# Seven tiles for raw weights in place of three, and one weight load ahead of queries and keys

## The chip, the cores and the metric

One core of a Trainium2 chip runs the whole kernel in one launch. The metric is the device time of a launch in microseconds (us); a lower time is better. The engines are named as in the profile: PE (TensorE matmul), PEld (its weight load), DVE (VectorE), ACT (ScalarE), POOL (GpSimd) and SP (SyncE, which here only issues DMAs).

## The reference, cut to what matters

```python
x = attention(rotate(q), rotate(k), v)        # 4 batches, 8 heads, 576 tokens, 64 wide
x = x.transpose(0, 2, 1, 3).reshape(2304, 512)
h = x @ w_in                                  # 512 x 2048, float64 in memory
x = np.maximum(0.01 * h, h) @ w_out           # 2048 x 512, float64 in memory
idx, gate = route(x, expert_emb, tau)         # one of 8 experts for each token
out = gate * (np.maximum(x @ w1[idx], 0) @ w2[idx])
```

The change concerns `w_in` and `w_out` alone: 16 MB of 64-bit numbers that must be turned into 32-bit ones and then into pairs of 16-bit halves (a high part and a low part) before the dense layer can use them.

## The kernel before, in words

**Stages.** Attention runs over 16 pairs of heads (`g`), nine steps each, 144 steps in all. In steps 0 to 35 (`g` below `WHOLE`, batch 0) a step works in 32 bits: DVE takes the row maximum (L621), ACT the exponential (L626), PE transposes the result (L645), ACT and DVE copy it out (L651, L655), PE multiplies it with the values (L679), and on some steps PE runs filler matmuls (`keep_warm`, L659). Steps 36 to 143 use 16-bit halves and the dense layer is worked in between: 72 units, each a first matmul (`m_s1`, L285), a leaky ReLU (L292 to L303) and a second matmul (`m_s2`, L315). A unit takes two steps, one in the order `ORDER_A`, one in `ORDER_B`. What is left of the dense layer after step 143 runs alone, and the experts follow.

**Weights.** `w_in` and `w_out` are cut into 16 slices of 1 MB (`slices`, L208), taken in turn from the two. A job `weights(i)` (L210) owns a home tile: it issues the slice's DMA on SP (L215 or L224), decodes with two ACT and two DVE pieces (`decode`, L198, L200, L202, L205), squares it on ACT (L230 or L219) and, for a slice of `w_in`, sums over partitions on PE (L191), takes a power of two on DVE (`_pow2`, L91 to L93) and makes the halves (ACT L236, DVE L238). A slice of `w_out` decodes into `wo32` instead and keeps no halves yet. Then the job takes the next slice into the same home, whose DMA waits until the last instruction on that home is done. There are `NW + 1` = 3 homes: two tiles `raw0`, `raw1`, and the tile that later holds `xT`. When all 16 are squared, `convert` (L242) finds the scale of `w_out`, sets `M.known`, and two jobs `parts` make the halves of `w_out` in eight parts (ACT L261, DVE L263). A unit of the dense layer waits for the parts that it reads (`m_ready`, L267), and the rows of attention are made into 16 bits (`x_done`, L718) only once `M.known` is set and the job on the `xT` home is done.

**Order.** The program order of every engine is written out by a planner at build time. Each engine works its own list in that order. Jobs yield pieces with a cost on ACT (`A`) or DVE (`V`); a step has a few slots, and a slot goes through the jobs in a fixed list: rows to finish, the preparation of the next pair of heads (`prep_whole`, `prep`), values, routing, then the weight jobs by index, then `parts`. Every step adds `RATE1` (A=2.4, V=2.7) to two budgets that are capped at 1.5 times that; a weight piece is planned only while its budget is above zero, and a slot takes no more pieces of an engine once 1.2 of cost are used. After a load, a job's first piece waits for two steps (`TICK`). In the steps of batch 0 a job may not go from ACT to DVE or back within a step. Before step 0 the planner runs six steps without attention (`PRE`), in which only weight work and the routing directions are planned; the rotation of the first queries and keys (`ropes`, L411) is planned at their start.

```python
    em = mp.tile([NE, DM], F32, name="em", tag="x2T", bufs=1)      # L770
    nc.sync.dma_start(out=em, in_=emb)
    for t in range(2):
        load(0, t)                          # queries, rotation table, keys, on SP
    nc.sync.dma_start(out=idn, in_=ident)
    end(load_values(0))                     # values, on SP
    nc.sync.dma_start(out=itau, in_=tau.to_broadcast([128, 1]))
...
    wjobs += [Job(weights(i)) for i in range(NW + 1)]              # L1215
    rjobs.append(Job(directions()))
    M.step = -1
    for _ in range(PRE):
        step(None)
    a_scores(0)
```

Of the kernel before, what the change touches and what calls it, by code (L numbers as in the profile page):

```python
# [9 lines left out]
F32 = mybir.dt.float32  # L10
# [4 lines left out]
U32 = mybir.dt.uint32  # L15
AF = mybir.ActivationFunctionType
# [19 lines left out]
XTB = 2  # L36
NW = 2
# [8 lines left out]
SPARE = 4  # L46
# [39 lines left out]

def _pow2(nc, pool, sq2, n, inv):

    t = pool.tile([128, n], U32, name="pt", tag=f"pt{n}")
    s = pool.tile([128, n], F32, name="ps", tag=f"ps{n}")  # L90
    nc.vector.tensor_scalar(out=t, in0=sq2.bitcast(U32), scalar1=0xFFFFFFFF, scalar2=24, op0=ALU.bitwise_xor, op1=ALU.logical_shift_right)  # L91
    nc.vector.tensor_scalar(out=s.bitcast(U32), in0=t, scalar1=-50.0, scalar2=2.0 ** 23, op0=ALU.add, op1=ALU.mult)
    nc.vector.tensor_scalar(out=inv.bitcast(U32), in0=t, scalar1=-2.0 ** 23, scalar2=304.0 * 2 ** 23, op0=ALU.mult, op1=ALU.add)  # L93
    return s
# [3 lines left out]
def attention_moe_kernel(ctx: ExitStack, tc: tile.TileContext, qkv, w_in, w_out, emb, tau, w1, w2,  # L98
                         rope, ident, tokc, iota, pcol, out):
    nc = tc.nc  # L100
# [5 lines left out]
    small = pool("small", 3)  # L106
# [40 lines left out]
    wo = wq.tile([128, 2, NF, DM], F16, name="wo")  # L147
    wo32 = wq.tile([128, NF, DM], F32, name="wo32")
    homes = [wp.tile([128, 2, 2048], F16, name=f"raw{i}") for i in range(NW)] + [mp.tile([128, 2, 2048], F16, name="xT", bufs=1)]
    blocks = []  # L150
    for b in range(B):
        blocks += [((b, 0), (b, 1)), ((b, 2), (b, 3))]
# [17 lines left out]
    M = Ctx()  # L170
# [13 lines left out]
    def cur_block():  # L184
        return munits[M.unit][0] if M.unit < len(munits) else len(blocks)
# [23 lines left out]

    def weights(i):  # L210
        raw = homes[i].rearrange("p a b -> p (a b)").bitcast(U32).rearrange("p (f t) -> p f t", t=2)
        while len(slices) > (SPARE if i >= NW else 0):
            f, o = slices.popleft()
            if o:
                nc.sync.dma_start(out=raw.rearrange("p (c f) t -> p c (f t)", c=2),  # L215
                                  in_=w_out32[256 * f:256 * f + 256, :].rearrange("(c p) f -> p c f", p=128))
                r = yield from decode(raw, wo32[:, 2 * f:2 * f + 2].rearrange("p c f -> p (c f)"))
                yield Piece(A=1.3)
                nc.scalar.activation(out=wo[:, 0, 2 * f:2 * f + 2].rearrange("p c f -> p (c f)"), in_=r, func=AF.Square, accum_out=uw[:, 1, f:f + 1])  # L219
                M.normed += 1  # L220
                if M.normed == NF // 2:
                    cjobs.append(Job(convert()))
            else:
                nc.sync.dma_start(out=raw.rearrange("p (c f) t -> p c (f t)", c=4),  # L224
                                  in_=w_in32[:, 512 * f:512 * f + 512].rearrange("(c p) f -> p c f", p=128))
                wv = (yield from decode(raw)).rearrange("p (c f) -> p c f", c=4)
                hi, lo = (wi[:, a, :, 256 * f:256 * f + 256] for a in range(2))
                sq = small.tile([128, 1], F32, name="wsq", bufs=NW + 1)
                yield Piece(A=1.3)
                nc.scalar.activation(out=lo, in_=wv, func=AF.Square, accum_out=sq)  # L230
                pb = yield from total(sq, 1)
                yield Piece(must=True, V=0.2)
                s = _pow2(nc, small, pb[:, 0:1], 1, uw[:, 0, f:f + 1])
                M.scaled.add(f)
                yield Piece(A=1.2)
                nc.scalar.activation(out=hi, in_=wv, func=AF.Copy, scale=s)  # L236
                yield Piece(V=1.28)
                nc.vector.scalar_tensor_tensor(out=lo, in0=wv, scalar=s, in1=hi, op0=ALU.mult, op1=ALU.subtract)  # L238
                M.wdone[0].update((2 * f, 2 * f + 1))
            yield Piece()  # L240
# [139 lines left out]
    def decoded():  # L380
        return not slices and not any(z.live for z in wjobs)
# [6 lines left out]
    pairs, values = {}, {}  # L388
# [9 lines left out]

    def load_values(g):
        yield Piece(at=9 * (g - 1) + LAG)  # L400
        v = values[g] = stp.tile([128, 1170], F32, name="v32", tag="v")[:, 0:650].rearrange("p (c h x) -> p c h x", c=5, h=2)
        nc.gpsimd.memset(v[:, :, :, 64:65], 1.0)
        nc.sync.dma_start(out=v[:, :, :, 0:64], in_=qkv[g, :, 2])
        yield Piece()
        if g + 1 < WHOLE:
            vjobs.append(Job(load_values(g + 1)))
        else:
            load(g + 1, 2)
# [309 lines left out]
    def x_done(b, c, x):  # L718

        ch = chunk[b, c]  # L720
        j = block_of[b, c]
        yield Piece(A=0.61, when=lambda: M.known and not any(z.live for z in wjobs[NW:]) and j < cur_block() + (2 * XTB if decoded() else XTB))
        sq = small.tile([128, 1], F32, name="xsq")
        nc.scalar.activation(out=junk[:, 0:512], in_=x, func=AF.Square, scale=2.0 ** 0.5, accum_out=sq, saturate=False)
        yield Piece(V=0.5)
# [43 lines left out]

    em = mp.tile([NE, DM], F32, name="em", tag="x2T", bufs=1)  # L770
    nc.sync.dma_start(out=em, in_=emb)
    for t in range(2):
        load(0, t)
    nc.sync.dma_start(out=idn, in_=ident)
# [437 lines left out]
            slot()  # L1212
            slot()

    wjobs += [Job(weights(i)) for i in range(NW + 1)]  # L1215
    rjobs.append(Job(directions()))
    M.step = -1
    for _ in range(PRE):
        step(None)
# [230 lines left out]
```

## Time and profile before

| | us |
|---|---|
| Median of 3 runs (996.04 to 997.65) | 997.16 |
| The profiled execution, its own time | 999.83 |
| Its span, first to last instruction | 998.0 |
| Start to the first row maximum (step 0, L621) | 37.52 |
| Step 0 to step 36 | 135.16 |
| Step 36 to step 76 | 164.30 |
| Step 76 to the last step, 143 | 267.71 |
| Dense layer alone, then experts | 122.06 and 271.25 |

The profile is of one execution. The span leaves out 1.83 us around it. The stages are cut at the start of a step's row maximum on DVE and read off the timeline; a busy window gives, for a stretch, the busy time of each engine, the TensorE clock granted (1.00 is 2.4 GHz, 0.50 is 1.2 GHz), and the DMA traffic. The name raw in a row stands for `raw0` and `raw1` alike. In a timeline row the brackets hold how long the engine stood idle before the instruction and what ended that.

### The profile page before, as it was taken

The numbers are of one execution on the slowest core, as the hardware profiler recorded it, in microseconds if no ns is written. First come the engines' busy times: TensorE is split into PE (matmuls) and PEld (weight loads), VectorE is DVE, ScalarE is ACT, GpSimd is POOL, SyncE is SP. The second block draws the span as 40 slices with busy tenths as digits, with TensorE's granted clock in tenths as the row PEclk, the third lists the DMA queues.
The fourth block names the chain that finished last, engine by engine and source line by source line (L and its number), as shares of the span: only waits on it lengthen the run. The fifth ranks groups of instructions, "written<-read, shape, count | busy, mean of one in ns | idle before, by whom it ended". The sixth has DMA issues, their size and how long they took to land. (4 is left out here: it accounts for less than half of the span.)

```text
span 998.0 us, 20007 instructions
## 1 busy us (share of the span) xinstructions
PE 908.3 (91%) x7414; PEld 690.6 (69%) x7414; DVE 770.8 (77%) x1601; ACT 671.3 (67%) x1033; POOL 125.5 (13%) x174
## 2 busy tenths in 40 slices
PE   2489888888998889998999999999998999999996
PEld 1377767555776667776677777767666788888885
DVE  4687788699889788888788766332668999999992
ACT  5688788476676676667676656333256998888882
POOL 0000000011201201201101100000013361211110
PEclk9999999799999899999999999999999999999999
DMA  6446333489879968988988854101341111115290
GB/s 208 140 153 208 97 100 76 83 144 173 164 128 149 174 114 154 183 134 142 155 139 138 153 80 81 47 22 33 128 148 44 63 43 43 43 62 193 63 342 20
DMA packets 215607, 118.87 MB, mean 119 GB/s; under 512 B 194727, under 2 KB 195175, under 8 KB 215504
## 3 DMA queue, kind: packets, MB, share of 16 engines
q1 hardware_dynamic: 205648, 84.54, 40.6%
q0 software_dynamic: 9856, 32.99, 12.2%
q8 instruction: 60, 0.98, 0.4%
q14 instruction: 43, 0.35, 0.1%
HBM read 120.04 MB, written 10.49 MB: 131 GB/s over the span
## 5 line engine op out<-in xcount | busy, mean ns | idle before, releaser
L285 PEld LDWEIGHTS <-wi 128*128 128x128 f16 x1920 | 172.6, 98 | 26.2 <-issue 2.7
L315 PE MATMUL acc<-wo,gh 128*128 128x512 f16 x576 | 140.9, 389 | 10.3 <-ACT gh L299 10.3
L292 ACT ACTIVATE g<-h 128x512 f32<-128x512 f32 x72 | 43.0, 598 | 127.5 <-PE h L285 53.8
L626 ACT ACTIVATE E<-E,amx 128x576 f32<-128x576 f32 x144 | 110.5, 767 | 23.8 <-DVE E L621 23.8
L285 PE MATMUL h<-xT,wi 128*128 128x256 f16 (+1 forms) x1152 | 114.4, 258 | 1.1 <-DMA xT<-x 1.1
L621 DVE TENSOR_SCALAR_CACHE_REDUCE E<-S,sc 128x576 f32<-128x576 f32 x108 | 87.9, 814 | 31.7 <-PE S L614 25.1
L315 PEld LDWEIGHTS <-gh 128*128 128x128 f16 x576 | 55.5, 100 | 69.5 <-ACT gh L299 13.0
L285 PE MATMUL h<-raw,wi 128*128 128x256 f16 x768 | 89.1, 273 | 0.0
L630 ACT ACTIVATE P<-E 128x576 f16<-128x576 f32 x108 | 74.0, 685 | 16.5 <-DMA PT<-P 13.3
L634 DVE SCALAR_TENSOR_TENSOR P<-E,P 128x576 f16<-128x576 f32 x108 | 81.1, 751 | 4.4 <-ACT P L630 3.9
L315 PE MATMUL acc<-wo,gl 128*128 128x512 f16 x288 | 76.5, 390 | 1.1 <-DVE gl L303 1.1
L679 PEld LDWEIGHTS <-PT 128*128 128x128 f16 (+1 forms) x1680 | 65.1, 101 | 17.5 <-issue 4.8
L295 DVE SCALAR_TENSOR_TENSOR g<-h,g 128x512 f32<-128x512 f32 x72 | 49.6, 688 | 28.7 <-ACT g L292 28.5
L612 PE MATMUL S<-stk 128*128 128x288 f16 (+1 forms) x240 | 59.0, 289 | 13.2 <-DVE E L621 12.8
L679 PE MATMUL o<-v,PT 128*128 128x65 f16 (+3 forms) x1680 | 69.3, 194 | 1.0 <-DMA PT<-P 1.0
L303 DVE TENSOR_TENSOR gl<-g,gh 128x512 f16<-128x512 f32 x72 | 49.5, 688 | 25.9 <-ACT gh L299 25.7
L1049 PE MATMUL h<-w,hth 128*128 128x512 f32 x176 | 55.4, 396 | 0.4 <-ACT hth L1033 0.4
L315 PEld LDWEIGHTS <-gl 128*128 128x128 f16 x288 | 28.9, 101 | 38.1 <-issue 3.3
L614 PE MATMUL S<-stk,raw 128*128 128x288 f16 (+1 forms) x220 | 52.7, 286 | 0.0
L299 ACT ACTIVATE gh<-g 128x512 f16<-128x512 f32 x72 | 44.5, 618 | 9.9 <-DVE g L295 9.8
L395 POOL DMA_DIRECT2D rawq<-in_qkv x15 | 8.5, 566 | 332.5 <-DVE stg L517 123.8
L983 DVE TENSOR_TENSOR w<-raw,w 128x1024 fp32r<-128x1024 f32 x40 | 46.3, 1221 | 3.5 <-ACT w L982 2.6
(301 smaller groups left out, 2015.7 us busy)
## 6 DMA issues: line engine op xcount, KB each, us to landing
raw<-in_w SPq DMA_DIRECT2D x78, 512.0 KB
ra<-in_w SPq DMA_DIRECT2D x76, 512.0 KB
raw<-in_w_out SPq DMA_DIRECT2D x7, 1024.0 KB
raw<-in_w_in SPq DMA_DIRECT2D x6, 1024.0 KB
rawq<-in_qkv POOLq DMA_DIRECT2D x15, 320.0 KB, 3.5
rawk<-in_qkv POOLq DMA_DIRECT2D x15, 320.0 KB, 6.5
x2s<-x POOLq DMA_DIRECT2D x18, 256.0 KB, 4.4
rawv<-in_qkv POOLq DMA_DIRECT2D x12, 320.0 KB, 3.7
```

The source lines that it names most:

```text
L285: nc.tensor.matmul(m.h[:, c0:c1], lhsT=wi[:, a, c, 128 * f:128 * f + 128], rhs=xT[j][:, 4 * b_ + c, 0:c1 - c0], start=(n == 0), stop=(n == ...
L295: nc.vector.scalar_tensor_tensor(out=m.g, in0=m.h, scalar=0.01 / TWO15, in1=m.g, op0=ALU.mult, op1=ALU.max)
L303: nc.vector.tensor_tensor(out=m.gl, in0=m.g, in1=m.gh, op=ALU.subtract)
L315: nc.tensor.matmul(M.acc[:, t], lhsT=g_[:, tt], rhs=wo[:, a, f], start=(f == 0 and n == 0), stop=(f == NF - 1 and n == 2))
L612: nc.tensor.matmul(ps[o:o + m, n, 0:288], lhsT=stk[:, h, c0:c0 + m], rhs=stk[:, 2 + h, ks], start=True, stop=False)
L614: nc.tensor.matmul(ps[o:o + m, n, 0:288], lhsT=pairs[g][3][:, h, c0:c0 + m], rhs=stk[:, 4, ks], start=False, stop=True)
L621: nc.vector.tensor_scalar(out=e[:, 0:S].rearrange("p (a b) -> p a b", a=2), in0=ps[:, :, 0:288], scalar1=-0.125 if g < WHOLE else pairs[g] ...
L626: nc.scalar.activation(out=e[:, 0:S], in_=e[:, 0:S], func=AF.Exp, scale=-1.0, bias=mx)
L630: nc.scalar.activation(out=p[:, 0:576], in_=e[:, 0:S], func=AF.Copy, scale=TWO15)
L634: nc.vector.scalar_tensor_tensor(out=p[:, 576:1152], in0=e[:, 0:S], scalar=TWO15, in1=p[:, 0:576], op0=ALU.mult, op1=ALU.subtract)
L679: nc.tensor.matmul(o[ob:ob + m, 256 * h:256 * h + r.shape[-1]], lhsT=pt[:, i, q0:q0 + m], rhs=r, start=(n == 0), stop=(n == len(todo) - 1))
L1049: nc.tensor.matmul(OP[kk], lhsT=h_[:, c, :], rhs=wt[a][c // 2][:, 512 * (c % 2):512 * (c % 2) + 512], start=(n == 0), stop=(n == len(todo) ...
```

## The change

- `homes` has seven tiles: the three of before and four views of `wo`, the tile in which the 16-bit halves of `w_out` are put later.
- The job on the first home is made, and its load issued on SP, ahead of queries, table and keys; its two ACT pieces are put at the head of ACT's list by two calls before the planner starts. The other six jobs are made where the three were.
- `x_done` waits for the job on the `xT` home alone, and that job alone stops when four slices are left (`SPARE`).
- The square of a `w_out` slice is written to the home itself and no longer to `wo`.
- The one-wide tiles of `_pow2` and the sum have eight buffers; the tile of the values in batch 0 is narrower (1040 in place of 1170).

```diff
+    kw = dict(bufs=8) if n == 1 else {}
+    t = pool.tile([128, n], U32, name="pt", tag=f"pt{n}", **kw)
+    s = pool.tile([128, n], F32, name="ps", tag=f"ps{n}", **kw)
...
+    homes += [wo[:, a, 8 * z:8 * z + 8].rearrange("p (x f) d -> p x (f d)", x=2) for a in range(2) for z in range(2)]
...
-        while len(slices) > (SPARE if i >= NW else 0):
+        while len(slices) > (SPARE if i == NW else 0):
...
-                nc.scalar.activation(out=wo[:, 0, 2 * f:2 * f + 2].rearrange("p c f -> p (c f)"), in_=r, func=AF.Square, accum_out=uw[:, 1, f:f + 1])
+                nc.scalar.activation(out=homes[i][:, 0, 0:1024], in_=r, func=AF.Square, accum_out=uw[:, 1, f:f + 1])
...
-                sq = small.tile([128, 1], F32, name="wsq", bufs=NW + 1)
+                sq = small.tile([128, 1], F32, name="wsq", bufs=8)
...
-        v = values[g] = stp.tile([128, 1170], F32, name="v32", tag="v")[:, 0:650].rearrange("p (c h x) -> p c h x", c=5, h=2)
+        v = values[g] = stp.tile([128, 1040], F32, name="v32", tag="v")[:, 0:650].rearrange("p (c h x) -> p c h x", c=5, h=2)
...
-        yield Piece(A=0.61, when=lambda: M.known and not any(z.live for z in wjobs[NW:]) and j < cur_block() + (2 * XTB if decoded() else XTB))
+        yield Piece(A=0.61, when=lambda: M.known and not wjobs[NW].live and j < cur_block() + (2 * XTB if decoded() else XTB))
...
     nc.sync.dma_start(out=em, in_=emb)
+    wjobs.append(Job(weights(0)))
     for t in range(2):
         load(0, t)
...
-    wjobs += [Job(weights(i)) for i in range(NW + 1)]
+    wjobs += [Job(weights(i)) for i in range(1, len(homes))]
     rjobs.append(Job(directions()))
+    for _ in range(2):
+        wjobs[0].run()
     M.step = -1
```

## Rows read from the trace of the kernel before

**Rows 1.** The page's busy time by engine (us, share of span, instructions).
```profile
PE 908.3 (91%) x7414; PEld 690.6 (69%) x7414; DVE 770.8 (77%) x1601; ACT 671.3 (67%) x1033; POOL 125.5 (13%) x174
```

**Rows 2.** Busy windows by stage: from:to length, busy by engine, granted clock, DMA share, GB/s.
```profile
37.52:172.68 135.16, 115.04 (x909) 96.03 (x909) 111.74 (x284) 110.69 (x165) 6.93 (x16) 0.97 0.41 127
172.68:263.13 90.45, 78.51 (x720) 53.24 (x720) 77.90 (x186) 55.84 (x90) 9.26 (x19) 0.91 0.74 126
263.13:336.98 73.85, 68.50 (x695) 48.66 (x694) 63.65 (x161) 51.38 (x92) 9.51 (x19) 0.95 0.87 157
336.98:604.69 267.71, 258.65 (x2740) 190.05 (x2737) 221.77 (x538) 177.69 (x305) 29.57 (x59) 0.99 0.82 140
604.69:726.75 122.06, 122.06 (x1039) 87.33 (x1038) 54.28 (x148) 43.59 (x79) 6.50 (x10) 1.00 0.23 63
```

**Rows 3.** Timeline of ACT before step 0: start, length, what.
```profile
12.60 1.13 ACT L198 ACTIVATE raw<-raw 128x1024 f32<-128x1024 f32 x1 [0.35 <-DMA raw<-in_w_in]
15.19 1.12 ACT L198 ACTIVATE raw<-raw 128x1024 f32<-128x1024 f32 x1 [1.46 <-DMA raw<-in_w_out]
...
30.17 1.13 ACT L198 ACTIVATE raw<-raw 128x1024 f32<-128x1024 f32 x1 [3.17 <-DMA raw<-in_w_out]
32.84 1.13 ACT L198 ACTIVATE raw<-raw 128x1024 f32<-128x1024 f32 x1 [1.54 <-DMA raw<-in_w_in]
```

**Rows 4.** Timeline of DVE before step 0 and at it.
```profile
5.04 0.89 DVE L417 TENSOR_TENSOR t<-rawq,tab 128x320 f32<-128x320 f32 x2 [1.31 <-DMA tab<-in_rope]
...
10.16 0.46 DVE L757 TENSOR_SCALAR em<-em,en 8x512 f32<-8x512 f32 x1
...
36.38 1.23 DVE L205 SCALAR_TENSOR_TENSOR wo<-raw 128x1024 uint32<-128x1024 uint32 x1
37.52 0.75 DVE L621 TENSOR_SCALAR_CACHE_REDUCE E<-S 128x576 f32<-128x576 f32 x1
```

**Rows 5.** Timeline of SP's DMA issues: the first weight load and the first reload.
```profile
4.64 0.44 SPq L224 DMA_DIRECT2D raw<-in_w_in  x1
...
25.19 0.37 SPq L215 DMA_DIRECT2D raw<-in_w_out  x1
```

**Rows 6.** Busy windows of one microsecond while weights load and at its end.
```profile
12.00:13.00 1.00, 0.29 (x3) 0.20 (x2) 0.19 (x1) 0.65 (x2) 1.00 (x2) 1.00 0.99 399
...
17.00:18.00 1.00, 0.00 (x0) 0.00 (x0) 0.54 (x1) 1.00 (x2) 0.00 (x0) 1.00 0.40 156
```

**Rows 7.** By line, decode pieces: ns min/median/max, first and last start in us.
```profile
L198 ACT ACTIVATE raw<-raw x13: 1118/1158/1207, 12.6 to 139.2; 128x1024 f32<-128x1024 f32 x13
L200 ACT ACTIVATE raw<-raw,half x13: 1208/1218/1261, 16.2 to 142.5; 128x1024 uint32<-128x1024 uint32 x13
L202 DVE SCALAR_TENSOR_TENSOR raw<-raw x13: 1218/1223/1244, 17.5 to 145.6; 128x1024 uint32<-128x1024 uint32 x13
```

**Rows 8.** Busy windows of three single steps in batch 0.
```profile
64.16:69.50 5.34, 4.38 (x33) 3.44 (x33) 5.27 (x14) 5.19 (x8) 0.00 (x0) 1.00 0.20 78
77.43:80.02 2.59, 2.59 (x27) 2.47 (x26) 2.52 (x9) 1.46 (x3) 0.00 (x0) 1.00 0.93 280
109.36:114.73 5.37, 5.37 (x41) 4.38 (x41) 1.48 (x8) 3.59 (x7) 0.00 (x0) 0.68 0.81 240
```

**Rows 9.** By line, the squares of w_out's slices and the eight parts.
```profile
L219 ACT ACTIVATE wo<-wo x8: 1042/1047/1052, 23.7 to 153.2; 128x1024 f16<-128x1024 f32 x8
L261 ACT ACTIVATE wo<-wo,uw x8: 1134/1136/1137, 158.9 to 231.2; 128x1024 f16<-128x1024 f32 x8
L263 DVE SCALAR_TENSOR_TENSOR wo<-wo,uw,wo x8: 1276/1278/1285, 162.2 to 236.3; 128x1024 f16<-128x1024 f32 x8
```

**Rows 10.** Busy windows at half clock and at an undisturbed pace, and the first dense unit.
```profile
171.00:184.70 13.70, 12.61 (x60) 9.17 (x61) 8.92 (x27) 6.80 (x13) 0.00 (x0) 0.50 0.22 42
...
263.13:313.74 50.61, 50.61 (x520) 37.15 (x519) 44.02 (x106) 35.46 (x63) 7.62 (x15) 1.00 0.94 163
...
178.89 5.28 PE L285 MATMUL h<-xT,wi 128*128 128x256 f16 x24 [1.09 <-DMA xT<-x]
```

More of the change, by code (lines that the diff above doesn't have):

```diff
@@ L87, in _pow2 @@
 def _pow2(nc, pool, sq2, n, inv):
-    t = pool.tile([128, n], U32, name="pt", tag=f"pt{n}")
-    s = pool.tile([128, n], F32, name="ps", tag=f"ps{n}")
+    kw = dict(bufs=8) if n == 1 else {}
+    t = pool.tile([128, n], U32, name="pt", tag=f"pt{n}", **kw)
+    s = pool.tile([128, n], F32, name="ps", tag=f"ps{n}", **kw)
     nc.vector.tensor_scalar(out=t, in0=sq2.bitcast(U32), scalar1=0xFFFFFFFF, scalar2=24, op0=ALU.bitwise_xor, op1=ALU.logical_shift_right)
```

## The prediction, made before the changed kernel was run

> **What bounds the kernel now.** I read the busy table first: PE is busy 91% of the span [rows 1]. That mean hides stages, so the busy windows by stage come next [rows 2]. From 336.98 us to 726.75 PE is busy 97 to 100% at a granted clock of 0.99 to 1.00; there only less PE work would help, and the change removes none. Before that no engine is full: from step 0 to step 36 (135.16 us) DVE is busy 111.74, ACT 110.69 and PE 115.04, and from 172.68 to 336.98 PE stands idle 17.3 us. The change acts on these early stages and on the 37.52 us ahead of step 0.
>
> Ahead of step 0 the timelines show a queue. ACT takes the first decode at 12.60, when the first tile has landed, and the second at 15.19; then the second round, into the same tiles, at 30.17 and 32.84, each time after waiting for a DMA [rows 3]. DVE must finish that round's two decode pieces, the last at 36.38, before it reaches the first row maximum at 37.52 [rows 4]. So the start ends on a reload: SP could issue it only at 25.19, when the first slice's low half was made [rows 5].
>
> **Part 1, the early load: queries come later.** The 1 MB load moves ahead of em's followers on SP. Two tiles of 1 MB landed 2.67 us apart (32.84 - 30.17) and 2.59 apart (15.19 - 12.60) [rows 3], at about 400 GB/s [rows 6], so queries and table land some 2.6 us later, and the issue itself takes 0.44 [rows 5]: the rotation starts near 7.75 in place of 5.04. It lasts to 10.16 and the two small pieces behind it to 10.6 [rows 4], so DVE is free for weights at about 13.4. The decode of the first tile on ACT (landing near 6.1, two pieces of 1.16 and 1.22 [rows 7]) ends by 8.5 and costs nothing: ACT then waits for the rotation anyway. But its DVE pieces stand behind the rotation and begin at 13.4, against 17.5 without the change [rows 7]. Bounds: 0.44 us if the loads shared the bandwidth so that the queries lost only the issue, 3.1 if both terms hold in full; the landings one behind the other in [rows 3] put me at 2.7. This cost is inside the next part's sum, since the start ends on something else.
>
> **Part 2, the start ends on the reload still.** I went through the planner's six steps by hand, budget by budget; for the kernel before this gives 12 ACT pieces and the order seen in the trace. For the new one it gives 14 ACT pieces (two unpaid, by the early calls) and 11 long DVE pieces in place of 9. The jobs are taken by index, so jobs 0 and 1, whose first slices are done in the third planner step, load a second slice and have it decoded in the fifth and sixth, ahead of the four new tiles that lie ready. That reload stands in SP's and the DMA queue's order behind seven tiles. The three tiles of before were through at about 18.5, by the traffic that falls from 399 to 156 GB/s [rows 6]; four more at 2.63 us each end at 29.1. The two reloads, issued near 27.9 (25.19 and the rotation's 2.7), then land at about 32.4 and 35.0, against 30.17 and 32.84 [rows 3]. Behind the second landing come one ACT piece of 1.16, and two of 1.22 of which the DVE pieces follow: four DVE pieces of 1.22 [rows 7] where two stood. So 35.0 + 1.16 + 1.22 + 4 x 1.22 = 42.3, against 37.52: **+4.8 us** to the first row maximum. Low bound +2.4 (landings as before, two DVE pieces more), high +6.5 (the queries' delay moves the reload's issue too).
>
> **Part 3, the steps of batch 0.** There are 56 ACT pieces for weights; 42 are left after the start in place of 44, and 29 of 40 long DVE pieces in place of 31. With three homes the gates of a job (two steps after a load, no change of engine within a step) spread them to step 31; the last square of before is at 153 us [rows 9]. With seven homes a piece is nearly always ready, and the ACT budget decides: 42 pieces at 1.21 and three preparations at 1.6 are 56 of cost, at 2.4 a step 23 steps. Without its 44 pieces and five parts of w_out at 1.14 ACT has 54.8 us of other work in 36 steps, 1.5 a step; DVE without 31 pieces at 1.2 and two parts has 72, 2.0 a step [rows 2, 9]. So for 23 steps ACT carries 1.5 + 42 x 1.14 / 23 = 3.6 and DVE 2.0 + 29 x 1.2 / 23 = 3.5. Where both are loaded a step lasts what the fuller one needs (5.34 for 5.27 and 5.19), and where neither is, PE sets 2.6 [rows 8]. Both swing from step to step, so I take 3.9: 90 us. In the other 13 steps all eight parts of w_out are made (before: only two of the DVE parts before step 36), at some 3.2 us of DVE work a step; I take 3.6, 47 us. Together 137 against 135.16: **+2**. Low bound: each step as long as its fuller mean, 23 x 3.6 + 13 x 3.3 = 126, -9. High bound: the 7 us more of DVE work at the ratio of before, 135.16 / 111.74 = 1.21, +8.5.
>
> **Part 4, steps 36 to 76.** Here the change gives back. Six DVE parts of 1.28 and four ACT parts of 1.14 leave this stage [rows 9], the last of them at 236. The units that waited for them run earlier: at one unit for two steps, eleven by step 58 in place of nine. But batch 0 has only 16 units, and the next rows of attention come when batch 1 is done, so units that run early leave steps without a unit near step 70. An undisturbed stretch with a unit every two steps takes 50.61 / 13 = 3.89 a step, all PE [rows 10]. Steps 36 to 58 at that pace are 85.6, plus about 3 for the half clock at their start, 88.5 against 90.45 [rows 2]. Steps 58 to 76 with five units in place of seven: ten at 3.89, three at 3.1, four with preparation and 16-bit rows at 3.9, one at 3.7 and 3 lost to the clock are 70.5 against 73.85. Together **-5**. Low bound -11 (all DVE parts and the 3.4 us), high bound 0 (PE work is unchanged).
>
> **Edits at nothing.** The buffers of the one-wide tiles and the narrower values tile issue the same instructions. The square into the home ends a reload's wait on ACT instead of DVE, about 1 us, but the job asks for the reload only after the square, and SP stands behind an earlier reload then; without that cover it is 1 us on SP. The zero-padded queries may be used from pair 4: four memsets move forward, which are in part 3.
>
> **Sum.** 4.8 + 2 - 5 = +1.8. Against the profiled execution's 999.83 (span 998.0 and 1.83 around it) that is 1001.6; the median of the runs is 2.67 lower, so I forecast **999.0 us**, on the edge of what a measurement can tell from no change (0.2%, 2.0 us).
>
> **Rivals.**
> *Packed steps (990, chance 0.24, faster).* If the 23 loaded steps take 3.6 and not 3.9, and the others 3.3, part 3 is -9 and the sum 997.2 + 4.8 - 9 - 5 = 988; half of the way to it still gives 992. For it: the steps in which both engines are loaded lose under 0.1 us [rows 8]. Against: steps of 2.59 and 5.34 some twelve us apart show how far the load swings.
> *Starved steps (1006, chance 0.13, slower).* Part 3 at its high bound: 997.2 + 4.8 + 8.5 - 5. It decides where loaded steps pass 4.2 us.
> *The clock at the change of stage (993, chance 0.10, faster).* From 171.00 to 184.70 the granted clock is 0.50, and the first unit takes 5.28 us there after waiting 1.09 for its rows [rows 10]; the clock fell in the last steps of batch 0, in which DVE and ACT set the pace. If rows and parts that are ready early keep PE busy, that stretch goes: up to half of its 12.61 us of PE work, 6.3 more, 999 - 6.
> *The parts stay late (1004, chance 0.06, slower).* The change does not do what it says: the new homes wait behind jobs 0 to 2, the last slice is squared near step 31 as before, part 4 gives nothing.
> *The clock in batch 0 (1030, chance 0.03, slower).* A step at a clock of 0.68 took 5.37 us, PE full [rows 8]; if most of the 23 loaded steps ran so, 23 x (5.37 - 3.9) = 34 us. The rows speak against: the mean clock of this stage is 0.97 [rows 2]. The Trainium skill, "TensorE: Matmul & The Clock Gate", section "Part 4: PE-mode transpose", says that transposes do not count as busy PE for the full clock; by it steps full of transposes and stretched by ACT work would lose the clock. The trace holds the full clock through such steps, so I give it little.
>
> **How the numbers follow.** My forecast has 0.44, with 995 to 1004 as its own range: 0.20 of it within 0.2% and 0.24 above. Faster: 0.24 + 0.10 = 0.34. Slower: 0.24 + 0.13 + 0.06 + 0.03 = 0.46. The range 988 to 1008 takes in the low and high bounds of part 3 with the other parts at their values, and leaves out the clock in batch 0 and the ends at which several bounds fall together.
>
> **What would show it.** Right: first row maximum at 41 to 43.5 with ACT waiting near 32 and 35 for raw; the last square near step 24; every L263 before step 36; units every second step from 37 on and a gap near step 70. Wrong: a first row maximum before 38 (part 2), step 36 more than 9 us from 137 after step 0 (part 3), or step 76 less than 153 or more than 165 us after step 36 (part 4).

## The result and the profile after

The changed kernel took **1011.78 us** (median of 4 runs, 1005.6 to 1015.95) beside 996.96 for the kernel before (4 runs, 996.04 to 997.65): ratio 1.0134, 95% interval 1.01 to 1.0169. That is 3.8 us above the predicted range. Three later sets with more runs gave less; both belong to the result:

| Set | before: runs, median | changed: runs, median | ratio (95%) |
|---|---|---|---|
| the result | 4, 996.96 | 4, 1011.78 | 1.0134 (1.01 to 1.0169) |
| f1_after_again | 31, 999.17 | 10, 1002.1 | 1.0029 (0.999 to 1.0068) |
| g1_after_third | 27, 1000.14 | 12, 1002.31 | 1.0024 (0.9991 to 1.0057) |
| h1_after_fourth | 23, 997.55 | 12, 1004.42 | 1.0064 (1.0034 to 1.0094) |

So by the ratios 34 later runs put the change at 2.4 to 6.4 us slower, inside the range, and the kernel before itself ran from 991 to 1008 us in these sets. The first four runs of the kernel before (996.04 to 997.65) were too narrow a sample of it. Why the first four of the changed kernel fell so high stays open.

The page's busy line and the stage windows of the profiled execution (1015.95 us, the highest of the four), cut at the row maxima of steps 0, 36, 76 and 143 as in [rows 2] (the line numbers from L151 on are two higher than before):

```profile
PE 908.2 (90%) x7414; PEld 693.7 (68%) x7414; DVE 770.2 (76%) x1601; ACT 669.6 (66%) x1033; POOL 126.6 (12%) x176
```

```profile
42.54:188.87 146.33, 122.82 (x919) 101.57 (x920) 117.58 (x290) 113.55 (x167) 7.97 (x18) 0.89 0.30 90
188.87:344.68 155.81, 139.86 (x1422) 101.72 (x1420) 133.24 (x338) 102.46 (x176) 19.16 (x39) 0.96 0.82 147
344.68:617.63 272.95, 257.44 (x2741) 188.79 (x2740) 221.94 (x538) 176.66 (x305) 28.91 (x58) 0.99 0.78 138
```

The instructions are those of [rows 1], with two more on POOL, and the busy times agree within 3.1 us; what moved are their places. Steps 0 to 36 are 11.2 us longer, at a granted clock of 0.89 where [rows 2] have 0.97, and steps 36 to 76 are 8.5 shorter. One profile is one execution, so the next table sets six beside each other (us). "Half clock" is the time in steps 0 to 36 at the 1.2 GHz level, worked out from windows of 2 us, the first and last cut at the ends of the stage, as twice the share by which the granted clock is below 1.00.

| Profile | to step 0 | 0 to 36 | half clock in it | 36 to 76 | 76 to 143 | after 143 | span |
|---|---|---|---|---|---|---|---|
| before | 37.52 | 135.16 | 8.5 | 164.30 | 267.71 | 393.3 | 998.0 |
| before (g4_before_look) | 37.36 | 135.72 | 10.2 | 164.43 | 268.14 | 393.3 | 998.9 |
| changed, the result | 42.54 | 146.33 | 31.0 | 155.81 | 272.95 | 396.5 | 1014.1 |
| changed (f1_after_again) | 42.47 | 143.19 | 17.0 | 157.72 | 260.41 | 394.5 | 998.3 |
| changed (g1_after_third) | 42.55 | 139.72 | 18.2 | 156.71 | 265.24 | 396.3 | 1000.5 |
| changed (h1_after_fourth) | 42.31 | 146.24 | 30.9 | 156.17 | 262.32 | 393.0 | 1000.0 |
| difference of the means | +5.0 | +8.4 | +14.9 | -7.8 | -2.7 | +1.8 | +4.8 |

**The start.** Timeline of the changed kernel ahead of step 0: the two reloads on ACT, the last weight pieces and the row maximum on DVE, the issues of the reloads on SP; they answer to [rows 3 to 5].

```profile
32.85 1.10 ACT L200 ACTIVATE raw<-raw 128x1024 f32<-128x1024 f32 x1 [4.66 <-DMA raw<-in_w_out]
35.53 1.10 ACT L200 ACTIVATE raw<-raw 128x1024 f32<-128x1024 f32 x1 [1.58 <-DMA raw<-in_w_in]
...
40.14 1.22 DVE L204 SCALAR_TENSOR_TENSOR raw<-raw 128x1024 uint32<-128x1024 uint32 x1
41.40 1.23 DVE L207 SCALAR_TENSOR_TENSOR raw<-raw 128x1024 uint32<-128x1024 uint32 x1
42.54 0.75 DVE L623 TENSOR_SCALAR_CACHE_REDUCE E<-S 128x576 f32<-128x576 f32 x1
...
27.40 0.37 SPq L217 DMA_DIRECT2D raw<-in_w_out  x1
```

ACT still ends the start on two reloads, and the row maximum comes at 42.54, where the prediction had 42.3.

**The weights.** By line in the changed kernel, the squares of w_out's slices and the eight parts, which answer to [rows 9]: the last of these squares starts at 132.2 in place of 153.2, and all parts lie before step 36 (188.87).

```profile
L221 ACT ACTIVATE raw<-wo x4: 1040/1044/1127, 25.9 to 128.5; 128x1024 f16<-128x1024 f32 x4
...
L221 ACT ACTIVATE wo<-wo x3: 1040/1040/1044, 83.3 to 132.2; 128x1024 f16<-128x1024 f32 x3
```

```profile
L265 DVE SCALAR_TENSOR_TENSOR wo<-wo,uw,wo x8: 1267/1276/1280, 154.9 to 179.7; 128x1024 f16<-128x1024 f32 x8
```

**The steps one by one.** Row maxima read off the timelines give the length of each step. Most are the same to 0.02 us in all four profiles of the changed kernel; in steps 0 to 36 eight differ by more than 0.1, and six of them carry most of it. Their lengths in us, with the granted clock of the step in brackets:

| Step | the result | f1 | g1 | h1 |
|---|---|---|---|---|
| 3 | 6.12 (0.78) | 3.60 (1.00) | 3.26 (1.00) | 6.09 (0.79) |
| 8 | 4.61 (0.63) | 4.63 (0.64) | 3.38 (1.00) | 4.61 (0.63) |
| 16 | 9.38 (0.53) | 6.99 (0.82) | 6.98 (0.85) | 9.38 (0.53) |
| 21 | 4.63 (0.63) | 3.09 (1.00) | 3.09 (1.00) | 4.64 (0.63) |
| 30 | 3.07 (1.00) | 4.68 (0.54) | 3.07 (1.00) | 3.07 (1.00) |
| 32 | 2.99 (1.00) | 4.53 (0.77) | 2.99 (1.00) | 2.99 (1.00) |

The instructions are the same in all four, and each step is long where its clock is low. With the smallest value of each step the 36 add up to 138.1 us (before, from its two profiles, 134.9). Above that the two profiles with 31 us of half clock have 8.1 and 8.2 us, f1 with 17.0 us has 5.1, and g1 with 18.2 has 1.6. So the half clock costs by where it falls: steps 0 and 1 ran at 0.50 in g1 and at 1.00 in f1, and both ended 7.9 us after the first row maximum.

Windows of the changed kernel (the result's profile): the 12 us up to shortly before step 16, and step 16 itself, then step 16 in g1; the columns are those of [rows 2].

```profile
93.00:105.00 12.00, 9.37 (x72) 7.53 (x71) 9.77 (x26) 11.39 (x17) 0.51 (x2) 0.97 0.56 173
...
105.67:115.05 9.38, 9.38 (x47) 7.19 (x46) 4.93 (x10) 5.03 (x8) 0.00 (x0) 0.53 0.00 0
...
103.04:110.02 6.98, 6.79 (x50) 5.28 (x50) 4.85 (x11) 5.41 (x8) 0.00 (x0) 0.85 0.00 0
```

The result's PE timeline there: a probability-times-values group, nine fillers, the next group and a score group, all at nearly twice the length they have at a clock of 1.00.

```profile
104.04 2.22 PE L681 MATMUL o<-v,ET 128*128 128x65 f32 x10
106.06 2.12 PE L661 MATMUL h<-ones 128*128 128x256 f16 x9
...
109.05 2.23 PE L681 MATMUL o<-v,ET 128*128 128x65 f32 x10
111.21 2.19 PE L599 MATMUL S<-qk 64*64 64x288 f32 x8
```

PE stood idle 2.6 of the 12 us ahead of it, mostly waiting for ACT, which was busy 11.39 of 12; then the granted clock fell, and a step in which ACT and DVE had 5 us of work each took 9.38, PE full.

### The profile page after: what moved, and what is told of

It is laid out like the page before. It is cut to its first block, busy times and chain, and to the rows that moved or that the text cites. A ratio compares the mean times of both kernels' runs of the same rounds, so it can differ in the third digit from the quotient of the medians.

```text
span 1014.1 us, 20013 instructions
## 1 busy us (share of the span) xinstructions
PE 908.2 (90%) x7414; PEld 693.7 (68%) x7414; DVE 770.2 (76%) x1601; ACT 669.6 (66%) x1033; POOL 126.6 (12%) x176
## 4 chain that ended last, share of the span: by engine, by line
PE 53%; DVE 16%; issue 13%; DMA 11%; ACT 6%; POOL 0%; SPq 0%; POOLq 0%; DVEq 0%; ACTq 0%
PE acc L317 15%; PE h L287 15%; PE o L681 5%; DMA out<-eo,idi 5%; PE S L1018 4%; PE h L1052 3%; DVE E L623 3%; PE S L614 2%; DMA PT<-P 2%; PE S L616 2%; DMA raw<-x 2%; PE S L599 2%; DMA xT<-x 1%; PE t L369 1%; DVE raw L204 1%
## 5 line engine op out<-in xcount | busy, mean ns | idle before, releaser
L614 PE MATMUL S<-stk 128*128 128x288 f16 (+1 forms) x240 | 58.4, 291 | 11.3 <-DVE E L623 11.2
L616 PE MATMUL S<-stk,raw 128*128 128x288 f16 (+1 forms) x240 | 58.1, 289 | 0.0
```

The costliest lines, as they stand in the source:

```text
L614: nc.tensor.matmul(ps[o:o + m, n, 0:288], lhsT=stk[:, h, c0:c0 + m], rhs=stk[:, 2 + h, ks], start=True, stop=False)
L616: nc.tensor.matmul(ps[o:o + m, n, 0:288], lhsT=pairs[g][3][:, h, c0:c0 + m], rhs=stk[:, 4, ks], start=False, stop=True)
```

## The experiments

Theory A: the clock, as PE stands idle for denser weight work on ACT and DVE. Theory B: the load itself, each stage as long as the work put into it. Theory C: the early load and the reloads ahead of ready tiles. The short edits are against the changed kernel where nothing else is said.

### The two parts alone: e1_homes_only, e2_early_only

```diff
# e1_homes_only
-    wjobs.append(Job(weights(0)))
...
-    wjobs += [Job(weights(i)) for i in range(1, len(homes))]
+    wjobs += [Job(weights(i)) for i in range(len(homes))]
...
-    for _ in range(2):
-        wjobs[0].run()
# e2_early_only, against the kernel before: the reverse of these, with three homes
```

> The seven homes without the early load: the first weight load stands behind queries, keys, identity and values again, as in the kernel before. Theory A (the clock: with a tile always ready, ACT and DVE take weight pieces in every step, PE stands idle for them, its clock falls to half and transposes then run long): steps 0 to 36 stay at 140 to 147 us with half-clock stretches among them; the start gets back 2 to 4 of its 5 us; total 1004 to 1010. Theory B (the load itself: loaded steps last what the fuller of ACT and DVE needs, at either clock): steps 0 to 36 the same 140 to 147, and their length follows ACT's and DVE's busy time and not the clock. Theory C (the early load and the reloads ahead of ready tiles do the harm): steps 0 to 36 fall below 140, total below 1003.

> The kernel before with the early load alone: three homes, the first tile loaded ahead of queries and keys and decoded at once. Theories A and B (the seven homes do the harm in batch 0): first row maximum at 39 to 41.5, steps 0 to 36 within 3 us of 135, total 998 to 1002. Theory C (the early load does it): total 1005 or more. A gain (below 995) would say that the early decode is worth its 2.6 us of later queries.

Measured: e1 1001.94 us, 1.0025 (0.9996 to 1.0053); row maximum at 39.30, steps 0 to 36 144.84 (half clock 28.8), 36 to 76 158.54. e2 1001.9 us, 1.0044 (1.0006 to 1.0082); 42.07, 139.44 (13.6) and 159.12. So of the start's 5.0 us the early load alone costs 4.6 (42.07 against 37.52) and the homes alone 1.8. In steps 0 to 36 the homes alone add 9.4 us to the 135.4 of before and the early load alone 4.0, one profile each, and g1 of the changed kernel itself has 139.72: the homes carry the long steps mostly, not alone. e2's 139.44 lies outside the 3 us around 135 that A and B gave it. A and B foretold the same here, so e1 and e2 don't tell them apart, and A's total for e1 (1004 to 1010) was too high; C holds for the start.

e2 also shortens steps 36 to 76 by 5.2 us, with three homes and the parts as late as before ([rows 9] have 236.3 for the last). Its parts by line, and the window of the stage, whose clock is 0.97 where [rows 2] have 0.91 and 0.95:

```profile
L263 DVE SCALAR_TENSOR_TENSOR wo<-wo,uw,wo x8: 1274/1277/1285, 167.7 to 238.2; 128x1024 f16<-128x1024 f32 x8
```

```profile
181.51:340.63 159.12, 143.40 (x1425) 101.82 (x1425) 140.51 (x346) 106.04 (x180) 19.27 (x39) 0.97 0.80 143
```

So a stage like this can be 5 us shorter with no part moved: 10 us of half clock are in it, 22 in the profile of before.

The start of e2 corrects my working. Timeline of e2, the first reload on ACT and its issue on SP, and its window ahead of that issue (last column GB/s):

```profile
32.40 1.11 ACT L198 ACTIVATE raw<-raw 128x1024 f32<-128x1024 f32 x1 [4.24 <-DMA raw<-in_w_out]
...
27.40 0.37 SPq L215 DMA_DIRECT2D raw<-in_w_out  x1
```

```profile
24.00:27.00 3.00, 0.00 (x0) 0.00 (x0) 2.80 (x6) 2.24 (x4) 0.00 (x0) 1.00 0.00 0
```

With three homes the queue is empty, yet the reload lands 5.0 us after its issue, as in the kernel before (25.19 to 30.17) [rows 3, 5] and nearly as behind seven tiles (27.40 to 32.85). The reload is late because its issue waits for the first slice's DVE pieces, the last of which ends at 27.37 (26.09 + 1.28) in the changed kernel, behind the later rotation; the four tiles ahead of it cost 0.45 us. The Trainium skill, "DMA: Bandwidth & Descriptors", section "Anatomy of one DMA", gives (for POOL's path) about 2.0 us fixed and the rest at 436 GB/s; for 1 MB that makes an estimate of 4.4 us, and the trace shows 5.0 on SP's.

### The sum a step later: e3_sum_later, f3_weight_sum_later

```diff
-        yield Piece(x=True)
+        yield Piece(x=True, tick=M.tick + 2)     # e3: every sum; f3: a weight slice's alone
         pb = ps_x()
```

> The changed kernel; the TensorE matmul that sums a slice's squares may go a step later, so that PE does not reach it before ACT has made the squares. Theory A: PE's waits for the squares (1 to 1.6 us each in batch 0) go, the clock stays up longer, steps 0 to 36 fall from 146 to 135 to 141, total 1000 to 1007. Theory B: ACT's and DVE's work is the same, steps 0 to 36 stay within 2 us of 146, total 1010 to 1014; a job now takes a step more for each slice of w_in, which could add up to 2 us.

> The changed kernel; only the sum over a weight slice's squares goes two planner steps after the squares in place of one; the sums of the later attention stages stay where they were. Theory A: steps 0 to 36 at 136 to 142 as with all sums later (140.3), the later stages as in the changed kernel, total 1001 to 1006 against the changed kernel of the same set. Theory B: steps 0 to 36 within 2 us of the changed kernel of the same set, total the same within 2 us.

Measured: e3 1068.55 us, 1.0721 (1.0631 to 1.0811): the edit also moved the sums in the preparation of every later pair, and steps 36 to 76 and 76 to 143 grew to 173.19 and 310.93. Its steps 0 to 36 took 140.30 us, which g1 of the changed kernel has without the edit. f3 1002.51 us, 1.0024 (0.999 to 1.0058) beside f1's 1.0029: steps 0 to 36 took 147.38 us with 33.7 us of half clock. PE's waits for the squares, in the changed kernel's steps 0 to 36

```profile
PE t L193 <- ACT wi L232: 2.8, 3, 1.4
```

(us in all, times, longest) are gone from f3's list of waits, and others grew in their place, this one from 2.8 us:

```profile
PE h L661 <- ACT ET L653: 7.7, 7, 4.4
```

So this form of theory A falls: the wait for the sum is one place where PE meets ACT's full list, and without it PE waits at the next.

### More fillers: f4_fillers_odd

```diff
-                    keep_warm(0 if units[i][1] in (1, 3, 5, 8) else WARM // 2 if units[i][1] == 7 else WARM)
+                    keep_warm(WARM // 2 if units[i][1] in (1, 3, 5, 8) else WARM // 2 if units[i][1] == 7 else WARM)
```

> The changed kernel with four filler matmuls more in each second step of batch 0 (20 steps, 80 matmuls, about 8 us of PE work at full clock). Theory A: PE stands idle less ahead of the transposes, the granted clock of steps 0 to 36 rises above 0.95 from 0.89, and steps 0 to 36 get shorter or stay, 138 to 146, in spite of the added work. Theory B: PE's added work lies in its idle time in part and lengthens the steps in which PE is full: steps 0 to 36 grow by 2 to 8 us, to 148 to 154; total 2 to 8 us above the changed kernel of the same set.

Measured: 1004.72 us, 1.0063 (1.0024 to 1.0103). Steps 0 to 36: 140.72 us, half clock 10.8 in place of 17 to 31, granted clock 0.96, with 64 matmuls more (16 steps have them; the expectation counted 20). Timeline and window of f4 around step 16, which took 5.33 us:

```profile
102.97 0.60 PE L647 MATMUL h<-idn,E 128*128 128x128 f32 x4
103.41 0.27 PE L647 MATMUL S<-idn,E 128*128 128x128 f32 x1
103.52 1.23 PE L681 MATMUL o<-v,ET 128*128 128x65 f32 x10
```

```profile
100.00:110.00 10.00, 8.97 (x73) 7.47 (x73) 9.14 (x29) 9.15 (x14) 0.00 (x0) 1.00 0.18 72
```

A group of ten takes 1.23 us here and 2.23 in the profile above. Steps 3, 8 and 21 took 3.51, 3.57 and 3.48 us, all at 1.00 and, with four fillers more in each, 0.2 to 0.4 above the shortest of the table. So theory A holds for these steps: it is the clock that makes 9.38 of 5.33. As a remedy the fillers failed: steps 36 to 76 took 162.25 us, with 23.9 us of half clock there, and the total did not fall.

### The budget: g2_rate_low

```diff
-RATE1 = dict(A=2.4, V=2.7)
+RATE1 = dict(A=2.1, V=2.4)
```

> The changed kernel with a lower budget for weight pieces in batch 0 (2.1 for ACT and 2.4 for DVE a step in place of 2.4 and 2.7): the eight parts of w_out then come at steps 34 to 52, as in the kernel before, and no longer at steps 28 to 35. Theory B (the length of a stage follows the work of ACT and DVE put into it): steps 0 to 36 fall by 4 to 6 us, to 137 to 140, steps 36 to 76 grow by 4 to 8, to 161 to 165, total within 3 us of the changed kernel of the same set. Theory A (the clock): the half clock in steps 0 to 36 falls below 12 us in place of 17 to 30, and total is 3 to 6 us lower. Packed steps (an earlier start of the units gains more than the denser steps cost) would make it 3 to 6 us slower.

Measured: 1002.53 us, 1.0028 (0.9999 to 1.0058), beside g1's 1.0024. Its two stage windows:

```profile
42.21:178.22 136.01, 117.16 (x911) 97.66 (x912) 109.42 (x283) 109.16 (x164) 6.92 (x16) 0.96 0.32 96
178.22:342.84 164.62, 145.67 (x1383) 101.50 (x1383) 140.15 (x344) 104.96 (x176) 18.17 (x37) 0.91 0.79 138
```

With the eight parts back behind step 34 the two stages are nearly those of the kernel before (135.2 and 164.3), and the total is the same, as theory B has it. But the half clock went with them: 11 us in steps 0 to 36, which was theory A's sign, and 30 us in steps 36 to 76, where the changed kernel has 14 to 20. So g2 doesn't tell load and clock apart. The seven homes move some 8 us from one stage to the other and gain nothing by it.

### The same kernels again: f1_after_again, g1_after_third, h1_after_fourth, g4_before_look

No edit.

> The changed kernel itself once more, with more runs and beside 25 or so of the kernel before, which in the first set of experiments ran from 991 to 1011 us (median 1000.1) and not only from 996 to 998. If the four runs of the result were a fair sample, its median is at 1009 to 1014 and the ratio 1.008 to 1.015. If its scatter comes from the clock and four runs fell high, the median is at 1003 to 1008. Steps 0 to 36 of the new profile: 140 to 148 us with half-clock stretches at about the same steps (theory A, since the order of instructions and PE's waits are fixed), or elsewhere, if the clock falls at random.

> The changed kernel once more, in more rounds. Four runs gave a ratio of 1.0134 (1.01 to 1.0169), ten later ones 1.0029 (0.999 to 1.0068). If the second set is the fairer sample, the ratio is at 1.000 to 1.006, a difference of 1 to 6 us; if the two sets differ by chip, this third one may fall at either. In the new profile the start is at 42.5 us and steps 0 to 76 together at 300 to 303 (both fixed by the order of instructions and the clock's usual losses), and what scatters by more than 3 us between profiles lies behind step 76.

> The kernel before, one more profile. If its steps 0 to 36 at 135.2 us with 9.8 us of half clock were the usual case, they are at 133 to 137 again; if that profile was a lucky one, at 138 to 141, with half clock of 15 us or more. The first row maximum stays at 37.5 within 0.2, and what scatters by more than 3 us lies behind step 76.

> The changed kernel in a fourth set. If the two sets of ten and twelve runs are the usual case: ratio 1.000 to 1.006. If the first four runs show a case that some chips or loads give: 1.009 to 1.015. Start at 42.5 us and steps 0 to 76 at 296 to 303 in the profile.

Measured: the two tables above. The kernel before repeats its stages within 0.6 us, so its 135.16 was no lucky case. The expectation that only what lies behind step 76 scatters was wrong: steps 0 to 36 of the changed kernel scatter by 6.6 us. Behind step 76 the result has 12.5 us more than f1: 6.0 in step 78 (10.60 us against 4.62), which waits for a DMA, 2.2 in step 79 behind it, at a clock of 0.67, and 4.1 in steps 88 and 116; g1 loses its time in steps 76 and 77. The waits for that DMA in step 78, of the changed kernel in the result and in f1:

```profile
ACT x L732 <- DMA raw<-x: 7.1, 1, 7.1
```

```profile
ACT x L732 <- DMA raw<-x: 1.1, 1, 1.1
```

The kernel before waits 4.6 at the same place. Steps 78 and 79 and the 3.1 us of steps 0 to 36 make up 11.3 of the 15.8 us between these two profiles of one kernel.

### The start: e4_reload_later, f2_homes_reload_later, g3_start_short, h4_start_three

```diff
-        yield Piece(A=1.15, tick=M.tick + (TICK2 if M.unit else TICK))
+        yield Piece(A=1.15, tick=M.tick + (TICK2 if M.unit else TICK if M.tick < 1 else 4))   # all four
...
-PRE = 6
+PRE = 4        # g3; 3 in h4
# f2: also without the early load, as in e1
```

> The changed kernel; a reloaded tile may be decoded four planner steps after its load in place of two, so that ahead of step 0 tiles that lie ready go first and no reload is waited for. All theories: the first row maximum comes at 28 to 32 in place of 42.5, with ten long DVE weight pieces ahead of it. Theory A: the work left goes on in batch 0, steps 0 to 36 stay at 140 to 150 with half-clock stretches; total 997 to 1005. Theory B: steps 0 to 36 grow by what the start no longer holds and by waits for the two reloads, to 148 to 154; total 1003 to 1010. Theory C (the start carries the loss): total 995 to 1000, steps 0 to 36 not longer than 146.

> Seven homes, no early load, and a reload decoded four planner steps after its load. The first row maximum comes before 30 us: eight long DVE pieces ahead of it and no wait for a reload. Theory C (the early load costs the start its 2.6 to 3.5 us of later queries, in whatever combination): 3 to 5 us faster than the same kernel with the early load (993.1 us), 988 to 991. Theories A and B: what the start no longer holds is paid in batch 0, whose steps 0 to 36 grow to 142 to 148; total 992 to 998.

> The changed kernel with the reload decoded four planner steps after its load, and four planner steps ahead of step 0 in place of six: nine ACT and seven long DVE weight pieces ahead of the first row maximum, which comes at 27 to 29.5 us in place of 35.1. If batch 0 has room for the pieces (ACT and DVE are busy 113 to 118 of 140 us there), steps 0 to 76 grow by less than the 6 us gained, to 295 to 299, and the total is 988 to 992; if a moved piece costs there what it costs in the start, 993 to 996; if batch 0 is full, 997 or more.

> The changed kernel with the later reload and three planner steps ahead of step 0. The first row maximum at 26 to 29 us against 31.6 with four steps. Batch 0 then takes six pieces more than in the changed kernel on each engine; if it has room still: total 986 to 990; if it is full by now (143.5 us for steps 0 to 36 with four planner steps, against 140 with six): 991 to 995.

Measured (steps 0 to 36 with half clock in brackets):

| Kernel | us | ratio (95%) | to step 0 | 0 to 36 | 36 to 76 |
|---|---|---|---|---|---|
| e4 | 993.12 | 0.9961 (0.9924 to 0.9999) | 35.12 | 139.95 (17.0) | 155.03 |
| f2 | 996.81 | 0.9983 (0.9945 to 1.0021) | 32.13 | 141.31 (17.2) | 157.92 |
| g3 | 990.81 | 0.9902 (0.9867 to 0.9937) | 31.58 | 143.54 (23.9) | 157.87 |
| h4 | 990.13 | 0.9885 (0.9823 to 0.9948) | 27.59 | 139.47 (23.4) | 157.34 |

The starts of e4, f2 and g3 came 2 to 3 us later than I expected, since DVE waits for ACT and PE between the pieces ahead of step 0. e4's total lies below what any of the three theories said; C's 995 to 1000 was nearest. A piece moved out of the start costs little in batch 0: g3 starts 11 us before the changed kernel, and its steps 0 to 36 are as long as the four's mean (143.9), though 3.6 us longer than e4's, with 7 us more of half clock. This is where the loss of the change could be won back. e4 and f2 do not differ by more than their intervals, so theory C's 3 to 5 us for f2 did not show.

### What the homes are worth with a short start: h2_before_start_short, h3_homes_start_short, i1_best_again, i2_no_gate

```diff
# h2, against the kernel before
-PRE = 6
+PRE = 4
...
-RATE1 = dict(A=2.4, V=2.7)
+RATE1 = dict(A=2.8, V=3.1)
# h3 and i1 (one kernel): f2 with PRE = 4; i2: the same with e4's line as it was
```

> The kernel before, with three homes and no early load, four planner steps ahead of step 0 in place of six, and a higher budget in batch 0 (2.8 and 3.1) so that the weights are still done in time. The first row maximum comes at 25 to 27 us, 11 us earlier. Theory D (the start's reload is what costs, and the homes matter little): steps 0 to 76 grow by less than 5 us from 299.5, total 989 to 994. Theory E (three homes cannot feed batch 0 with four more pieces on each engine, seven can): steps 0 to 76 grow by 8 us or more, total 997 or more.

> Seven homes, no early load, the later reload, four planner steps ahead of step 0. The first row maximum at 24 to 27 us. If the early load is worth its later queries (a tile decoded while ACT stands idle, two DVE pieces more ahead of step 0), the total is 2 to 5 us above the same kernel with it (990.8); if it only delays the start, 986 to 989. Theory E would have it below the kernel before with the short start, theory D at the same time within 3 us.

> Seven homes, no early load, the later reload, four planner steps ahead of step 0, once more. If its four runs were a fair sample: ratio 0.983 to 0.991. If they fell low, as the changed kernel's four fell high: 0.990 to 0.995. First row maximum at 25.5 us within 0.2; steps 0 to 76 at 294 to 300.

> The same without the later reload: a reloaded tile may be decoded two planner steps after its load. The first row maximum stays at 25 to 26 us, since no reload is decoded ahead of step 0 with four planner steps; ACT then meets the first reload in steps 0 to 2 and may wait for it up to 3 us. If the pieces planned ahead of step 0 are what counts: within 3 us of i1. If the wait for the reload is what counts, wherever it stands: 3 to 6 us slower than i1.

Measured: h2 993.79 us, 0.9955 (0.9918 to 0.9993), row maximum at 27.87, steps 0 to 76 300.6. h3 983.29 us from four runs, 0.9874 (0.9805 to 0.9942); the same kernel as i1 988.61 us from seven, **0.9906 (0.9871 to 0.994)**, row maximum at 25.14, steps 0 to 76 301.4. i2 989.05 us, 0.9911 (0.9882 to 0.994). Steps 0 to 76 of h2 are 1.1 us longer than before, and its total is where theory D (the start's reload is what costs, the homes matter little) had it: with three homes too the shorter start is worth some 4 us. That seven homes without the early load gain some 5 more on top (0.9906 and 0.9911 against 0.9955) is not shown: the intervals overlap, and h2 has another budget too. i2's ACT waits for the first reload inside batch 0,

```profile
31.89 1.14 ACT L200 ACTIVATE raw<-raw 128x1024 f32<-128x1024 f32 x1 [2.86 <-DMA raw<-in_w_out]
```

and loses nothing measurable by it: it was the pieces planned ahead of step 0 that cost, not the reload's wait wherever it stands. i1 and i2 beat both the kernel before and the changed one. Whether the early load is worth anything here is not settled: g3 with it has 0.9902, i1 without it 0.9906.

## Why the prediction was right and wrong

**Part 1 and Part 2 (the start): right in size, one step of the working wrong.** +5.0 was measured where +4.8 stood; the rotation began at 8.51 where 7.75 stood, 3.5 us late and so beyond the high bound of 3.1. But "behind the four new tiles the reloads land at 32.4 and 35.0" was nearly the right number for the wrong reason, and so in part luck: e2's reloads land at 32.40 and 35.06 without those tiles, the changed kernel's at 32.85 and 35.53. A landing is its issue plus 5.0 us [rows 3, 5]; the issue moved by 2.2, and two long DVE pieces more stood ahead of the row maximum.

**Part 3 (batch 0): the step that failed.** Predicted +2 with 8.5 as high bound; measured +8.4 as the mean of four profiles and +11.2 in the one of the result. The shortest lengths of the steps add up to 138.1 against 134.9, +3.3, and that still holds step 16 at a clock of 0.85; with f4's 5.33 us for it, my estimate is +1.6 (before's 134.9 holds its own steps at 0.68 to 0.82). So the load itself was sized well at +2. The rest, 5 to 7 us, is the clock: it lies in the steps of the table, long where the clock is low, and the half clock grew from 9 to 24 us. The last square of w_out came in step 21, the last of all in step 23 (forecast 24). I had the mechanism among the rivals as *the clock in batch 0*, at 34 us and 0.03, as if the clock fell for all loaded steps or for none. It falls for a few: steps 3, 8, 16, 21. The sentence "the trace holds the full clock through such steps" rested on one loaded step at 1.00 and on the stage's mean of 0.97; rows 8 already had, beside it, a step at 0.68 that took 5.37 us with DVE busy 1.48. The right use of it was a term of a few us in the sum, and a range to match. The rule cited there, that transposes don't count for the full clock, was not put to the test: f4 added matmuls that are no transposes, and the clock held in steps 2 to 29, but more work of any kind might have held it too.

**Part 4 (steps 36 to 76): right in size, its cause shown only in part.** -5 with bounds -11 and 0; measured -7.8 as a mean, -8.5 in the result. The units run every second step from 193.56, the sixteenth at 310.42, and then none until 337.17, the gap near step 70. g2 gives it all back when the parts are late, but with 30 us of half clock in the stage; e2 gains 5.2 us with late parts and 10 us of half clock. Early parts against the clock: h1 has 156.17 us with 20 us of half clock, about as much as before has with its 164.3, so the parts are worth something by themselves; how the 7.8 divide stays open.

**The sum.** +1.8 was forecast. 34 later runs give 2.4 to 6.4, the four profiles +4.8. The first four runs give 14.8. The profiled one of them has +16.1 against the profile of before: 9.2 more than forecast in part 3, 3.5 less in part 4, 0.2 more at the start, and 8.4 behind step 76, which the sum put at nothing. It is 8 to 12.5 us above the other three profiles in steps 76 to 143, step 78's DMA among them, for which the prediction had nothing; whether the other three lost theirs there too was not seen, as they have no profile. My range ignored that one kernel's runs spread over 11 to 16 us within a set, because the three runs shown agreed within 1.6.

**The other rivals.** *Starved steps* (1006) has the stage's size, +8.4 for its +8.5, but the cause was the clock more than a load above 4.2 us a step. *Packed steps* fell. *The parts stay late* fell by [rows 9] and their rows after. *The clock at the change of stage*: the stretch of 13.7 us at 0.50 [rows 10] is not in the profile after, where 0.50 shows only at 193 to 196 and around 207 to 210; it may be part of Part 4's gain.

## What to carry to other kernels

Look at what stands ahead of the first step before adding to it: pieces planned there cost their full length, and the same pieces cost little in a stage whose engines are 80% busy; here that was worth 1%, and the change itself lost 0.2 to 0.6%. When work is packed denser on two engines that a third one waits for, price the third one's clock step by step, from the rows of before where it has fallen already. And profile the same kernel twice before trusting a range: steps that repeat to 0.02 us show what is fixed, and the few that don't show what scatters.

## What the runs showed of the hardware that was not expected

- **The granted clock differs between executions of the same instructions.** Windows of the changed kernel in the result and in g1, at the same place behind the same start:

```profile
44.00:50.00 6.00, 5.03 (x20) 3.58 (x21) 4.86 (x13) 5.67 (x9) 0.00 (x0) 0.50 0.55 175
50.00:56.00 6.00, 6.00 (x30) 5.47 (x29) 4.30 (x8) 3.93 (x5) 0.00 (x0) 0.50 0.35 93
```

```profile
44.00:50.00 6.00, 5.03 (x20) 3.57 (x21) 4.87 (x13) 5.67 (x9) 0.00 (x0) 0.50 0.56 175
50.00:56.00 6.00, 6.00 (x52) 5.50 (x50) 4.50 (x9) 5.30 (x8) 0.00 (x0) 0.96 0.33 89
```

  After an idle stretch PE starts at half clock in both, with the same 5.03 us of work in the first 6; in the next 6, PE full in both, one gets through 30 of its records and the other 52. In f1 the clock at the same place is 1.00 throughout. The Trainium skill, "TensorE: Matmul & The Clock Gate", section "Part 1: The HAM clock gate (the "warmup" mystery)", says that the gate judges activity on a clock of its own that does not start with the kernel, so that the same kernel runs a different number of slow matmuls each time; these rows agree. It calls the loss of the warm-up under 1% of a typical span; the scatter that went with the half clock in batch 0, 6.6 us in some 1000, is under 1% too, but more than the whole change was forecast to move.
- **A 1 MB load on SP's queue lands 5.0 us after its issue with the queue empty** (27.40 to 32.40 in e2) and 5.45 with the last of seven tiles still on its way (27.40 to 32.85; 389 GB/s from 26 to 27 us).
